# Four plain products ahead of the state products in the last batch's first attention chunk

## The chip, the cores and the metric

The kernel runs on one core of a Trainium2 chip. The metric is the device time of one execution in microseconds; "before" and "after" are two versions of the same kernel. The engines are called as in the profile: PE (TensorE, matrix products, with PEld for its weight loads), DVE (VectorE), ACT (ScalarE), POOL (GpSimd) and SP (SyncE, which here only issues DMAs). DMAs are issued from SP, ACT and POOL.

## The reference

Two blocks follow each other. First a causal linear attention with decay over 4 batches, 8 heads, 768 positions and head size 64, in which a state is carried from block to block:

```python
intra = einsum('bhic,bhjc->bhij', qb, kb) * Dmask        # scores, masked by lam ** (i - j)
intra = einsum('bhij,bhjd->bhid', intra, vb)
inter = einsum('bhid,bhde->bhie', qb * lam_pow, kv_state)
out[:, :, sl] = intra + inter
kv_state = lam_block * kv_state + einsum('bhsd,bhse->bhde', kb * rev_pow, vb)
```

The heads are joined to rows of 512. Then comes a Fourier mixing layer on these x (4 x 768 x 512), all in float32:

```python
mixed = real(fft(fft(x, axis=1), axis=2))
u = x + mixed
un = (u - mean(u)) / sqrt(var(u) + 1e-06)
return u + maximum(un @ w_ch1, 0) @ w_ch2                # 512 -> 2048 -> 512
```

## The kernel before

**Stages.** Each batch passes through a front: attention in six chunks of 128 rows (`attn`, with `attn_in` for loads and transposes and `attn_out` for the rest of a chunk), then `fft_ln`: folds of the rows with their mirrored rows on DVE, the transform along the sequence as products with a table (L516), the transform along the width (L529 to L534), the sum u (L599 to L603) and the normalization (`norm`, L546 to L577). The mirrored rows come back from DRAM by indirect DMAs: each chunk's rows x are stored from ACT (L365 to xa, L367 to xb), `mirror_a` and `mirror_b` gather them on POOL (L439, L445, L452).

**The plain feed-forward.** The normalized rows are handled in twelve pairs of 128-row tiles. The first four pairs (`PLAIN`) pass through `mlp`, the plain products: L636 is the first layer (eight or sixteen groups of four products into a PSUM bank), L644 on ACT or L642 on DVE the relu that empties the bank, L650 the second layer (for each of two tiles, eight or sixteen products accumulated in one bank), L661 and L662 on DVE add u and make y, and y goes to the output from SP (L623) or, for the mirrored tile, as a scatter from POOL (L625). PSUM has three banks for these (`pm`) and five for everything else (`pa`).

**The late pairs.** The other eight pairs are written to DRAM and handled at the end by `late`, with combined weights: `combine_weights` (L700, on DVE) forms sums of weight blocks, L713 to L716 those of the rows (us), L723 and L770 are the products and L750 to L762 and L736 to L743 the copies, sums and relus between them.

**The order of the work.** A part of the kernel is a Python generator that issues some instructions and then yields a number, its planned duration. `weave` runs a lead generator and, each time it yields d, issues work of the other generator until that one's planned time has caught up with a ratio of the lead's. So the number yielded decides how much plain work is issued at that place. In the last woven stretch the lead is the fronts of batches 1 to 3 (`fr`), and the other is the plain products left (`back`). A scheduler then sets the final order on each engine by readiness and issue order; `tc.keep_in_program_order(i)` holds an instruction at its place in the order of issue.

**The place of the change.** In `attn_out` the scores are L298 (k and q transposed, sixteen instructions), masked on DVE at L302 to sc, then comes `yield 1.5`. The state products are L315 (kd, made on POOL at L270, times v, into pu), copied or added to the state on DVE (L317, L320), then `yield 0.9`. Then po takes the state part (L328, not in chunk 0) and the scores part (L332, which reads sc). ACT copies po (L335), PE turns it (L348) and ACT copies it to x (L352, L353). In batch 3 (the last, B - 1) the plain products that lie beside chunks 0 and 1 are the L650 of the second pair's second half (`half[1][1]`, two tiles); beside chunks 2 to 5 lies the third pair's second half, and from there on the fourth pair.

Of the kernel before, what the change touches and what calls it, by code (L numbers as in the profile page):

```python
# [76 lines left out]
def kernel(  # L77
# [11 lines left out]
    B, H, S, D = q.shape  # L89
# [16 lines left out]
    HD = [slice(0, 64), slice(64, 128)]  # L106
# [36 lines left out]
    def psum_a(shape):  # L143
        return new(pa, shape, "pa")
# [101 lines left out]
    def attn(b):  # L246

        head = () if b - 1 in LEADS else attn_in(b, 0)
        for c in range(NC):
            yield from head  # L250
            head = attn_in(b, c + 1) if c < NC - 1 else attn_in(b + 1, 0) if b in LEADS else ()
            yield from attn_out(b, c, head)
# [36 lines left out]
    def attn_out(b, c, head):  # L289
        kT, qT, qs, kd, vt = ins.pop((b, c))  # L290
# [3 lines left out]
        mm = nc.tensor.matmul  # L294
# [8 lines left out]
            sc.append(t)  # L303
        if last and b - 1 in LEADS:
            mirror_a(b, pin=True)
        yield 1.5


        s_old, s_new = st[(c + 1) % 2], st[c % 2]
        if not last:  # L310
            pu = psum_a([128, HP, D])
            for hp in range(HP):
                for hi in range(2):
                    h = 2 * hp + hi
                    mm(pu[HD[hi], hp, :], lhsT=kd[:, h, :], rhs=vt[:, h, :], start=True, stop=True)  # L315
            if c == 0:
                nc.vector.tensor_copy(s_new, pu)  # L317
            else:
                nc.gpsimd.tensor_tensor(s_new, s_old, spow.broadcast_to([128, HP, D]), op=ALU.mult)
                nc.vector.tensor_tensor(s_new, s_new, pu, op=ALU.add)  # L320
            yield 0.9
# [3 lines left out]
        if c > 0:  # L325
            for hp in range(HP):
                for hi in range(2):
                    mm(po[HD[hi], hp, :], lhsT=s_old[HD[hi], hp, :], rhs=qs[HD[hi], hp, :],  # L328
                       start=(hp == 0), stop=False, skip_group_check=True)
        for hp in range(HP):  # L330
            for hi in range(2):
                mm(po[HD[hi], hp, :], lhsT=vt[:, 2 * hp + hi, :], rhs=sc[hi][:, hp, :],  # L332
                   start=(c == 0 and hp == 0), stop=(hp == HP - 1), skip_group_check=True)
# [99 lines left out]
    def mirror_a(b, pin=False):  # L433

        xa = xd[b][0]

        eo[b] = new_eo()
        for a, n in enumerate(BLK):
            i = gather(out=eo[b][a][1][0:n, 1, 0:DM], out_offset=None, in_=xa[:, :], in_offset=row_of(a, n))  # L439
            if pin:  # L440

                tc.keep_in_program_order(i)
        for t in range(2, HC):
            u = xs[b, HC + t] = new(xp, [128, DM], "x")
            i = gather(out=u[:, :], out_offset=None, in_=xa[:, :], in_offset=row_of(2 + t))  # L445
            if pin:
                tc.keep_in_program_order(i)
# [458 lines left out]
```

## Time and profile before

| | us |
|---|---|
| median of five runs | 822.7 (820.37 to 824.76) |
| profiled execution | 820.77 |
| its span, first to last instruction | 819.0 |
| PE busy in the span | 794.2 |
| DVE busy | 438.3 |
| ACT busy | 185.7 |
| POOL busy | 84.8 |

The granted TensorE clock was 0.999 of full speed over the span, so no part of the time is due to a slower clock. In the profile a line is that of the kernel before. The last batch's attention lies between about 286 and 357 us, its folds between 355 and 374, its transform and normalization up to about 420, and the late pairs from 428 to the end at 819. PE's float32 products are issued as two instructions each, with a weight load each; the counts in the profile are those of instructions. A row of a timeline gives its start, its length, engine, line, operation, output <- inputs, shape and count, and in brackets how long the engine stood idle before it and what ended that.

### The profile page before, as it was taken

The page shows a single profiled execution, that of the slowest core. Times are in us where ns is not written, and L with a number is a line of the kernel's source. Part 1 is how long each engine was busy: PE and PEld are TensorE (multiplying, and loading weights), DVE is VectorE, ACT ScalarE, POOL GpSimd, SP SyncE. Part 2 cuts the span into 40 slices and gives each one's busy share as a digit, 9 for nine tenths or more (in the row PEclk, how much of TensorE's full clock was granted, in tenths as well). Part 3 has the DMA queues.
Part 4 walks back from the last instruction along what each step waited for, and adds up shares of the span by engine and source line. Part 5 has one row for each costly group of instructions (what it writes and reads, how often), then busy time and mean ns, then how long its engine had stood idle before and what let it go on. Part 6 is the DMA issues. An engine that isn't in the chain of part 4 may idle for free.

```text
span 819.0 us, 11694 instructions
## 1 busy us (share of the span) xinstructions
PE 794.2 (97%) x4608; PEld 634.3 (77%) x4608; DVE 438.3 (54%) x1018; ACT 185.7 (23%) x448; POOL 84.8 (10%) x102
## 2 busy tenths in 40 slices
PE   6989899999999999999999999999999999999998
PEld 5767767767585857768648888888888888888886
DVE  6899798766743761364995541255313661146311
ACT  3755344225420211312002200022001210022100
POOL 3223340011011010220000000000000000000000
PEclk9999999999999999999999999999999999999999
DMA  9969524248741136530350011100111001110010
GB/s 253 258 126 274 171 90 129 65 117 200 198 125 51 53 63 130 130 122 26 94 165 38 1 53 51 52 1 1 64 40 52 0 1 39 33 33 0 1 39 26
DMA packets 126684, 68.88 MB, mean 84 GB/s; under 512 B 111150, under 2 KB 112174, under 8 KB 126630
## 3 DMA queue, kind: packets, MB, share of 16 engines
q1 hardware_dynamic: 121488, 55.67, 26.5%
q0 software_dynamic: 2112, 6.69, 2.4%
q10 hardware_dynamic: 3030, 5.78, 1.9%
q8 instruction: 36, 0.59, 0.3%
q14 instruction: 18, 0.15, 0.1%
HBM read 48.72 MB, written 19.40 MB: 83 GB/s over the span
## 4 chain that ended last, share of the span: by engine, by line
PE 80%; DVE 10%; issue 4%; DMA 3%; ACT 2%; POOL 1%; POOLq 0%; ACTq 0%; DVEq 0%
PE p L770 24%; PE p L723 24%; PE pm L650 10%; PE pm L636 8%; PE pa L332 3%; PE pa L516 3%; PE pa L298 2%; DMA x<-xb,ix 2%; PE pa L328 2%; PE pa L274 1%; PE pa L315 1%; DVE sc L302 1%; PE pa L348 1%; PE pa L279 1%; DVE stt L546 1%
## 5 line engine op out<-in xcount | busy, mean ns | idle before, releaser
L636 PE MATMUL pm<-ut,w 128*128 128x256 f32 x512 | 119.2, 382 | 0.0
L650 PE MATMUL pm<-w,hr 128*128 128x512 f32 x256 | 115.8, 597 | 0.1
L636 PEld LDWEIGHTS pm<-ut,w 128*128 128x128 f32 x512 | 94.4, 190 | 15.4 <-issue 3.6
L723 PE MATMUL p<-ur,w 128*128 128x256 f32 x384 | 93.8, 379 | 0.0
L650 PEld LDWEIGHTS pm<-w,hr 128*128 128x128 f32 x256 | 46.6, 190 | 49.5 <-issue 48.0
L723 PEld LDWEIGHTS p<-ur,w 128*128 128x128 f32 x384 | 73.0, 190 | 10.3 <-issue 0.5
L723 PE MATMUL p<-us,w1s 128*128 128x256 f32 x256 | 65.7, 379 | 0.0
L770 PE MATMUL p<-w,hs 128*128 128x256 f32 x256 | 58.0, 379 | 0.5 <-DVE y L791 0.5
L770 PE MATMUL p<-w2s,hs 128*128 128x256 f32 x256 | 57.9, 379 | 0.0
L770 PE MATMUL p<-w,ha 128*128 128x256 f32 x256 | 57.9, 379 | 0.0
L770 PEld LDWEIGHTS p<-w,hs 128*128 128x128 f32 x256 | 48.5, 190 | 7.5 <-DVE y L791 0.9
L770 PEld LDWEIGHTS p<-w2s,hs 128*128 128x128 f32 x256 | 48.6, 190 | 6.6
L723 PEld LDWEIGHTS p<-us,w1s 128*128 128x128 f32 x256 | 48.6, 190 | 6.6
L770 PEld LDWEIGHTS p<-w,ha 128*128 128x128 f32 x256 | 48.6, 190 | 6.6
L625 POOL DMA_INDIRECT out_dram<-y,ix x12 | 11.8, 987 | 402.0 <-DVE y L796 342.6
L750 ACT COPY ha<-p 128x256 f32<-128x256 f32 x32 | 11.9, 372 | 169.1 <-PE p L723 139.4
L761 DVE TENSOR_TENSOR ha<-p,ha 128x256 f32<-128x256 f32 x32 | 13.6, 424 | 45.2 <-ACT ha L760 45.2
L298 PEld LDWEIGHTS pa<-qT,kT 64*128 64x128 f32 x384 | 26.0, 193 | 13.2 <-ACT qT L281 7.2
L302 DVE TENSOR_TENSOR sc<-pa,decay 128x512 f32<-128x512 f32 x48 | 31.4, 682 | 8.9 <-PE pa L298 8.9
L332 PE MATMUL pa<-sc,v 128*64 128x128 f32 x384 | 31.5, 281 | 3.4 <-DVE sc L302 3.4
L298 PE MATMUL pa<-qT,kT 64*128 64x128 f32 x384 | 30.7, 292 | 3.2 <-ACT qT L281 2.9
L723 PE MATMUL p<-ur,w1s 128*128 128x256 f32 x128 | 32.8, 379 | 0.0
(144 smaller groups left out, 1123.4 us busy)
## 6 DMA issues: line engine op xcount, KB each, us to landing
raw<-in_moe_w_ch_dram SPq DMA_DIRECT2D x32, 512.0 KB, 4.3
k<-in_k_dram SPq DMA_DIRECT2D x24, 256.0 KB, 5.1
q<-in_q_dram SPq DMA_DIRECT2D x24, 256.0 KB, 5.8
v<-in_v_dram SPq DMA_DIRECT2D x24, 256.0 KB, 4.7
ud<-x SPq DMA_DIRECT2D x16, 256.0 KB, 2.3
utd<-e SPq DMA_DIRECT2D x64, 64.0 KB, 2.2
u<-ud SPq DMA_DIRECT2D x16, 256.0 KB, 2.5
ur<-utd SPq DMA_DIRECT2D x6, 512.0 KB, 3.7
```

The source lines that it names most:

```text
L298: mm(pss[hi][:, hp, :], lhsT=kT[HD[hi], hp, :], rhs=qT[HD[hi], hp, :], start=True, stop=True)
L302: nc.vector.tensor_tensor(t, pss[hi], decay[:, hi::2, :], op=ALU.mult)
L328: mm(po[HD[hi], hp, :], lhsT=s_old[HD[hi], hp, :], rhs=qs[HD[hi], hp, :], start=(hp == 0), stop=False, skip_group_check=True)
L332: mm(po[HD[hi], hp, :], lhsT=vt[:, 2 * hp + hi, :], rhs=sc[hi][:, hp, :], start=(c == 0 and hp == 0), stop=(hp == HP - 1), skip_group_chec ...
L516: mm = nc.tensor.matmul(ps[0:m, n, :], lhsT=piece(a, i, n), rhs=cs[0:rows, a, i in (2, 3), n, :], start=(a == 0), stop=(a == 1))
L625: nc.gpsimd.indirect_dma_start(out=out.rearrange("b s d -> (b s) d"), out_offset=row_of(2 + HC * (b + 1) + T - HC), in_=y[:, :], in_offset ...
L636: nc.tensor.matmul(ps, lhsT=w1[:, c, 128 * fc:128 * fc + 128], rhs=ut[:, c, :], start=(c == 0), stop=(c == KO - 1))
L650: nc.tensor.matmul(ps, lhsT=hr[(fc - f0) // 4][:, fc % 4, 128 * i:128 * i + 128], rhs=w2[:, fc, :], start=(fc == f0), stop=(fc == f1 - 1))
L723: nc.tensor.matmul(ps, lhsT=s2.A[a][:, kt, 128 * i:128 * i + 128], rhs=U[b][:, kt, :], start=(first and kt == 0), stop=(kt == 1), skip_gro ...
L750: nc.scalar.copy(a11, two(X))
L761: V.tensor_tensor(a22, two(Z), a22, op=ADD)
L770: nc.tensor.matmul(ps, lhsT=h[a][:, s, i, :], rhs=s2.B[b][:, i, :], start=(first and i == 0), stop=(i == HF - 1), skip_group_check=True)
```

## The change

The number yielded between scores and state products becomes 5.0 instead of 1.5 in chunk 0 of batch 3, and the first state product of that chunk is held at its place in the order of issue.

```diff
-        yield 1.5
+
+        yield 5.0 if (b, c) == (B - 1, 0) else 1.5
...
-                    mm(pu[HD[hi], hp, :], lhsT=kd[:, h, :], rhs=vt[:, h, :], start=True, stop=True)
+                    i = mm(pu[HD[hi], hp, :], lhsT=kd[:, h, :], rhs=vt[:, h, :], start=True, stop=True)
+                    if (b, c, h) == (B - 1, 0, 0):
+                        tc.keep_in_program_order(i)
```

In the built programs every engine issues the same instructions as before, and the order is the same up to this chunk. From here on it differs as follows (lines of the kernel before).

- PE: between L298 and L315 of chunk 0 stand seven products of L650 instead of three. In chunk 1, L315 comes ahead of four products of L650 instead of behind them, and none stand behind its L332. From there to the last L348 of the attention there are fourteen products of L650 instead of twelve, behind it two instead of four, then L636. Before the transform's products on the second block of rows stand 28 products of L636 instead of 23, and between the first of the three parts of the transform along the width and L723 there are 27 instead of 32.
- DVE: L661 and L662 of the second pair's first tile stand ahead of L317 of chunk 0, those of the third pair's first tile ahead of L285 of chunk 5, and those of its second tile ahead of the first eight folds (L426 to L430, on the rows that `mirror_a` gathers), each instead of behind.
- POOL: the scatter L625 of that last tile (the third pair's second) stands ahead of the two gathers L452 of batch 3 instead of behind them.
- ACT: one relu (L644) stands ahead of the copy L466 of the folds instead of behind it. SP: no difference.

## The prediction

> **What bounds the kernel now.** I read the page first: TensorE (PE) is busy nearly all the time and carries most of the chain that ended last, so a microsecond counts only if PE stands still in it, or if another engine holds up its last stage.
>
> ```profile
> PE 794.2 (97%) x4608; PEld 634.3 (77%) x4608; DVE 438.3 (54%) x1018; ACT 185.7 (23%) x448; POOL 84.8 (10%) x102
> PE 80%; DVE 10%; issue 4%; DMA 3%; ACT 2%; POOL 1%; POOLq 0%; ACTq 0%; DVEq 0%
> ```
>
> Next the PE timeline where batch 3's first chunk runs (start, length, instructions; a product counts as two):
>
> ```profile
> 288.98 2.84 PE L650 MATMUL pm<-w,hr 128*128 128x512 f32 x6
> 291.75 0.69 PE L315 MATMUL pa<-v,kd 128*64 128x64 f32 x16
> 294.01 0.43 PE L332 MATMUL pa<-sc,v 128*64 128x128 f32 x2 [1.58 <-DVE sc L302]
> ...
> 296.48 3.60 PE L650 MATMUL pm<-w,hr 128*128 128x512 f32 x8
> ```
>
> PE waits 1.58 us for the masked scores, which VectorE (DVE) finishes late. This is the largest such wait. The next PE wait is at 371.97, for the folds of batch 3 (0.96 us); behind it come the timelines of POOL, DVE and ACT:
>
> ```profile
> 114.47 6.21 POOL L452 DMA_INDIRECT x<-xb,ix  x1 [0.30 <-issue]
> ...
> 360.46 0.94 POOL L452 DMA_INDIRECT x<-xb,ix  x1 [4.83 <-DMA xb<-xn]
> 361.71 0.95 POOL L452 DMA_INDIRECT x<-xb,ix  x1 [0.30 <-issue]
> 362.96 0.99 POOL L625 DMA_INDIRECT out_dram<-y,ix  x1 [0.30 <-issue]
> ```
> ```profile
> 355.44 0.69 DVE L426 TENSOR_TENSOR fe<-fo,xn 128x512 f32<-128x512 f32 x1 [3.86 <-DMA fo<-xa,ix]
> 356.17 0.69 DVE L427 TENSOR_TENSOR fo<-fo,xn 128x512 f32<-128x512 f32 x1
> ...
> 363.70 0.69 DVE L426 TENSOR_TENSOR fe<-x,x 128x512 f32<-128x512 f32 x1 [2.54 <-DMA x<-xb,ix]
> ...
> 428.43 0.41 DVE L662 TENSOR_TENSOR y<-pm,x 128x256 f32<-128x256 f32 x1
> ```
> ```profile
> 428.85 0.37 ACT L750 COPY ha<-p 128x256 f32<-128x256 f32 x1 [29.72 <-DVE y L662]
> 429.72 0.42 DVE L752 TENSOR_TENSOR ha<-p,ha 128x256 f32<-128x256 f32 x1 [0.89 <-ACT ha L750]
> ```
>
> The last rows matter most. The first copy of the last stage (L750) starts when DVE has ended L662 (428.84), not when its PE bank is full; it ends at 429.22, and PE's first products with us, which write that bank again, start at 429.46. PE has 0.24 us to spare. DVE has no pause to give: from 403.65 to 428.84 it is busy 25.15 of 25.19 us. So two chains of equal length meet here: PE's products, and gather, folds, transform, normalization and weight combinations, mostly on DVE. A stall filled on PE helps only if the second chain comes earlier too.
>
> **Step 1, the stall.** Four more products (eight instructions of 0.43 us) stand before L315. From the rows: 288.98 + 2.77 (six instructions) + 3.44 (eight more) puts L315 at 295.19, + 0.61 (its length at 305.17) L332 at 295.80. The masked scores end at 294.56, so the wait is gone; the last of the four needs the relu that DVE ends at 293.36 and would start at 294.14, so it does not wait either. Then 1.03 for L332 and 0.49 + 0.44 for the transposes, now uninterrupted: the next L650 at 297.76. Before, PE had done the same work at 296.48 + 3.44 = 299.92: 2.16 ahead, 1.58 of the wait and 0.58 of the split runs. With the same rows for chunk 1, whose state products L315 now stand ahead of its plain ones, L636 comes at 309.00 instead of 311.36: 2.36 ahead. POOL's kd for chunk 1 follows L315 and would be ready at about 297, needed at 302.8; the L317 copy moves behind y (about 297.6, needed at 307): both are covered by products.
>
> **Step 2, more products before the last chunk's store.** The weave hands out plain work earlier from here on. As built, 14 and not 12 L650 products lie between chunk 1 and the last L348: + 1.72. The last L348 comes at 356.32 - 2.36 + 1.72 = 355.68, 0.64 earlier.
>
> **Step 3, queues.** SP's order does not change. On POOL the scatter L625 now stands before both L452 gathers, and on DVE L661/L662 (the y it waits for) before the first folds instead of after them. L661 waits for the last L650: 355.68 + 0.44 + 1.72 = 357.84; + 0.20, + 0.75: y ends at 358.79. The eight folds queued behind it start at about 358.71 (their gather, landed at 355.44 before, is long there), and take 4.08, as before: to 362.79. POOL starts L625 0.28 after y (326.46 to 326.75 before): 359.07. The gathers wait behind it, and DVE's second folds, and then PE, for them.
>
> Here is the cost that no row shows directly. Both POOL issues fall beside folds that read two SBUF tiles back to back. The nearest row is the 6.21 us at 114.47: DVE ran such instructions without a pause until L470 waited for ACT (119.77), and POOL ended 0.94 later, just one undisturbed issue. So POOL got in at DVE's first pause. The folds have one: L426 to L427 takes 0.73 (355.44 to 356.17), against 0.61 at 363.70. I take entry there, the row nearest in kind: L625 at 359.32, + 0.99 + 0.30 the gather asks at 360.61, inside the folds again, and enters at the second such pause, 361.33. Lower bound: no hold, 359.07 + 1.29 = 360.36; a row speaks for it too, since at 354.64 a POOL issue took 0.99 while L426 ran beside it, but POOL had begun first. Upper bound: held until the folds end, 362.79 + 1.29 = 364.08. The scatter's own transfer (3.2 from issue to landing) ahead of the gather's could add up to 0.3; I take none. Against 360.46 the gather is 0.87 later (-0.10 to +3.62).
>
> [...]
>
> **Step 4, folds to transform.** DVE's second folds start 3.24 after the gather, at 364.57. PE's L636 groups run dry of banks: the sixth waits for the L642 that DVE runs inside the folds, 4.33 after their start (368.90), while PE is there at 366.5: a new PE wait of about 2.4 us. It costs nothing by itself, as the folds would stop PE a group later anyway: L516 on the second block at 364.57 + 8.27 = 372.84 instead of 371.97. On ACT one more relu (L644) stands before the fold's small copy L466; PE has filled its bank by 363.1 and the copy is due at 366: covered. One more product of L516 stands behind the block (0.33): the transform hands over to DVE 1.2 later than at 384.01.
>
> **Step 5, the junction.** PE now has five L636 products (2.16) fewer between the transform and L723, so it is there 2.16 - 1.20 = 0.96 early and waits. DVE's chain has the same instructions in it and ends 1.2 later; less the 0.24 to spare, PE's first products with us start 0.96 later. Behind this nothing changes.
>
> Sum: 1.20 - 0.24 = +0.96, about +1.0 us. The profiled execution took 820.77 (span 819.0 and 1.8 around it), so 821.7 for its like; the median of the five runs is 1.9 higher, 822.7, which gives 823.7. About 0.3%, 2.5 us, can be told from no change, so this is "same".
>
> **Rivals.**
> - The folds do not hold POOL (chance 0.27): -0.10 + 0.01 + 0.33 - 0.24 = 0.0, 822.7. For it: the issue at 354.64. Against it: 114.47.
> - Slower, one mechanism (0.17): POOL gets no pause until the folds end. The gather is 3.62 late, + 0.33 - 0.24 = +3.7, 826.4. It exceeds 2.5 us once the gather starts later than 362.8. For it: 5.3 us without entry at 114.47. Against it: the 0.12 pause in the folds.
> - The stall does not go (0.05): the added products wait for their relu on DVE, busy with normalization just then. Without the 2.36 gained, everything is later: +3.3, 826.0.
> - Faster (0.06): PE's own chain decides, with L750 free of DVE. Both PE waits gone is 2.36 + 0.96 = 3.3, 819.4. Against it: if only the earlier store counted, the second chain would be 0.64 - 0.33 earlier, + 0.24: a gain of 0.55 at most while L750 waits for L662.
>
> **How the numbers follow.** The forecast has 0.45 and its own range 823.1 to 824.5 (entry one pause earlier or later, the scatter's 0.3). The medians themselves scatter by about 1 us (820.37 to 824.76 over five runs). The faster case and the tail below no change are left out, the held POOL is kept: 821.2 to 826.4. Held POOL, a stall that stays, less what of them stays under 2.5 us: slower 0.19; faster 0.06; the rest, 0.75, same.
>
> **What would show it.** Step 1: no wait for sc at L332, its start near 295.8, L636 near 309.0. Step 2: last L348 near 355.7. Step 3: L625 longer than 1.1 or late against y, the first L452 starting or ending after 361.5. Step 4: a PE wait before an L636 group near 366.5, L516 near 372.8. Step 5: PE idle before its third pair of L723, with L750 still released by L662. I am wrong if POOL's issues are 0.95 long and on time (then no change), if L625 or L452 lasts 4 us (then slower), or if L750 starts while DVE is still at L700.

## The result, and the profile after

The changed kernel takes 824.07 us (median of 33 runs, 821.49 to 827.59), the kernel before 821.97 (58 runs): ratio 1.0027, 95% interval 1.0018 to 1.0035. That is slower by some 2.2 us (2.1 between the medians), "same" by the 0.3% of the prediction, and within its range. The number was right to 0.4 us, but the loss is twice the +1.0 of the sum, and its place was not the one forecast.

In the new profile a line of `late` stands 3 higher than before: L723 is L726, L750 is L753, L662 is L665; L302 stays. The profiled execution took 824.51 us (span 822.7). Executions reach the last batch's first chunk at different times, so from here I count from the transposes of q ahead of it (L279), which stand at 286.49 before and 287.22 after, and call this t. The span ends at t = 532.51 before and 535.48 after: +2.97. Spans are given to 0.1 us, so differences between such ends hold to about 0.1.

Two rows of PE before the change, the point from which t counts and the beginning of the last stage, whose first two products (called X and Y below) stand in one row of eight instructions:

```profile
286.49 0.60 PE L279 MATMUL pa<-ident,q 128*128 128x128 f32 x4
...
427.74 1.89 PE L723 MATMUL p<-ur,w 128*128 128x256 f32 x8
```

The timeline of PE in the changed kernel (start, length, line, instructions, and in brackets the idle time ahead and what ended it):

```profile
287.22 0.60 PE L279 MATMUL pa<-ident,q 128*128 128x128 f32 x4
...
296.43 1.04 PE L335 MATMUL pa<-sc,v 128*64 128x128 f32 x16
...
369.15 1.99 PE L639 MATMUL pm<-ut,w 128*128 128x256 f32 x8 [1.65 <-DVE hr L645]
...
426.98 1.03 PE L726 MATMUL p<-ur,w 128*128 128x256 f32 x4
430.57 1.71 PE L726 MATMUL p<-ur,w 128*128 128x256 f32 x4 [2.56 <-DVE y L665]
432.07 1.91 PE L726 MATMUL p<-us,w1s 128*128 128x256 f32 x4
433.78 1.30 PE L726 MATMUL p<-ur,w 128*128 128x256 f32 x4
434.92 1.03 PE L726 MATMUL p<-us,w1s 128*128 128x256 f32 x4
```

Two things are to be seen. The wait for the scores is gone, and PE reaches the last stage (its first product, X) at t = 139.76 instead of 141.25, 1.49 earlier. But there its second product (Y, a12 times b21) stands still for 2.56 us, until DVE has ended the last plain y (L665). Then twelve instructions, which before took 0.86 us per four, take 4.35 instead of 2.59. The windows view of the same kernel tells why (window, its length, busy time of PE, PEld, DVE, ACT and POOL, then the granted clock):

```profile
430.60:430.80 0.20, 0.20 (x1) 0.20 (x2) 0.00 (x0) 0.00 (x0) 0.09 (x1) 1.00 0.78 287
430.80:431.00 0.20, 0.20 (x2) 0.17 (x2) 0.00 (x0) 0.00 (x0) 0.20 (x1) 0.80 1.07 420
431.00:434.20 3.20, 3.20 (x9) 2.46 (x8) 0.72 (x2) 0.18 (x1) 0.79 (x1) 0.50 0.75 291
434.20:434.40 0.20, 0.20 (x2) 0.19 (x1) 0.00 (x0) 0.20 (x1) 0.00 (x0) 0.67 0.00 0
```

The granted clock is 0.50 for 3.4 us, from about 430.9 to 434.3, right after the idle time. So +2.97 is 1.24 of wait (Y starts at t = 143.35; before it was 142.11, worked out as the start of the row of eight at 427.74 plus 0.86) and some 1.7 of half clock.

The timelines of POOL, DVE and ACT of the changed kernel, for steps 3 and 5:

```profile
359.94 1.19 POOL L628 DMA_INDIRECT out_dram<-y,ix  x1 [4.96 <-DMA xb<-xn]
361.43 1.08 POOL L455 DMA_INDIRECT x<-xb,ix  x1 [0.30 <-issue]
362.81 0.99 POOL L455 DMA_INDIRECT x<-xb,ix  x1 [0.30 <-issue]
```
```profile
364.77 0.69 DVE L429 TENSOR_TENSOR fe<-x,x 128x512 f32<-128x512 f32 x1 [1.13 <-DMA x<-xb,ix]
...
427.87 0.69 DVE L717 TENSOR_TENSOR us<-ur,us 128x512 f32<-128x512 f32 x1
...
430.01 0.41 DVE L665 TENSOR_TENSOR y<-pm,x 128x256 f32<-128x256 f32 x1
```
```profile
428.09 0.37 ACT L753 COPY ha<-p 128x256 f32<-128x256 f32 x1 [29.72 <-DMA out_dram<-y]
```

The scatter L628 is 1.19 long, not 0.99; the gather behind it starts at t = 74.21 instead of 73.97, the second folds at 77.55 instead of 77.21, and the last y ends at 143.20 instead of 142.35, 0.85 later. The copy L753 does not wait for y: it starts 1.11 after PE's first product, while DVE is still at L717.

### The profile page after: what moved, and what is told of

Its sections match the earlier page's. It is cut to its first block, busy times and chain, and to the rows that moved or that the text cites. A ratio compares the mean times of both kernels' runs of the same rounds, so it can differ in the third digit from the quotient of the medians.

```text
span 822.7 us, 11692 instructions
## 1 busy us (share of the span) xinstructions
PE 795.3 (97%) x4608; PEld 635.2 (77%) x4608; DVE 438.0 (53%) x1018; ACT 186.6 (23%) x448; POOL 85.2 (10%) x102
## 5 line engine op out<-in xcount | busy, mean ns | idle before, releaser
L639 PE MATMUL pm<-ut,w 128*128 128x256 f32 x512 | 119.2, 383 | 1.7 <-DVE hr L645 1.7
L639 PEld LDWEIGHTS pm<-ut,w 128*128 128x128 f32 x512 | 94.3, 190 | 16.8 <-issue 2.9
L726 PE MATMUL p<-ur,w 128*128 128x256 f32 x384 | 94.9, 382 | 2.6 <-DVE y L665 2.6
L726 PEld LDWEIGHTS p<-ur,w 128*128 128x128 f32 x384 | 73.5, 191 | 13.5 <-issue 3.4
L726 PE MATMUL p<-us,w1s 128*128 128x256 f32 x256 | 66.6, 383 | 0.0
L726 PEld LDWEIGHTS p<-us,w1s 128*128 128x128 f32 x256 | 49.2, 192 | 6.9
L628 POOL DMA_INDIRECT out_dram<-y,ix x12 | 12.1, 1007 | 406.1 <-DVE y L799 343.6
L753 ACT COPY ha<-p 128x256 f32<-128x256 f32 x32 | 11.9, 372 | 169.1 <-PE p L726 139.4
L302 DVE TENSOR_TENSOR sc<-pa,decay 128x512 f32<-128x512 f32 x48 | 31.4, 682 | 13.6 <-PE pa L298 13.6
L298 PEld LDWEIGHTS pa<-qT,kT 64*128 64x128 f32 x384 | 26.0, 193 | 13.2 <-ACT qT L281 7.2
L298 PE MATMUL pa<-qT,kT 64*128 64x128 f32 x384 | 30.7, 292 | 3.2 <-ACT qT L281 2.9
L270 POOL TENSOR_TENSOR kd<-k,decay 128x512 f32<-128x512 f32 x20 | 23.1, 1155 | 99.1 <-PE pa L316 59.8
L335 PE MATMUL pa<-sc,v 128*64 128x128 f32 x384 | 31.1, 280 | 1.8 <-DVE sc L302 1.8
```

Source lines behind the costliest of these rows:

```text
L270: nc.gpsimd.tensor_tensor(kd, kt, kpow, op=ALU.mult)
L298: mm(pss[hi][:, hp, :], lhsT=kT[HD[hi], hp, :], rhs=qT[HD[hi], hp, :], start=True, stop=True)
L302: nc.vector.tensor_tensor(t, pss[hi], decay[:, hi::2, :], op=ALU.mult)
L628: nc.gpsimd.indirect_dma_start(out=out.rearrange("b s d -> (b s) d"), out_offset=row_of(2 + HC * (b + 1) + T - HC), in_=y[:, :], in_offset ...
L639: nc.tensor.matmul(ps, lhsT=w1[:, c, 128 * fc:128 * fc + 128], rhs=ut[:, c, :], start=(c == 0), stop=(c == KO - 1))
L726: nc.tensor.matmul(ps, lhsT=s2.A[a][:, kt, 128 * i:128 * i + 128], rhs=U[b][:, kt, :], start=(first and kt == 0), stop=(kt == 1), skip_gro ...
```

## The experiments

My theory was now: (A) the changed order turns the three `pm` banks so that Y gets the bank which the last y is read from, PE waits there, and the clock falls behind the wait. In the built kernels, before: the last plain product stands in bank 6, Y takes bank 7 and Z, later, bank 6; after: the last plain product and Y both have bank 7. The last stage takes banks 0, 7 and 6 in both; it is the last plain tile that has moved. Rivals: (B) DVE's lateness, from the scatter ahead of the gathers, sets the end whatever the bank; (C) the half clock has nothing to do with the wait.

**The bank alone.** A tile that takes bank 7 for itself, ahead of Y:

```diff
+            if (i, j) == (0, 0):
+                V.memset(bank()[0:1, 0:1], 0.0)
             prod(Y, "a12", "b21", i, True)
```

> The changed kernel with one thing more: a one-element memset takes the PSUM bank that the last plain tile's y is read from, so that the second product of the last stage (Y, L726) gets another bank. Theory A (that bank and the fall of the clock behind the wait for it make the loss): no idle time of TensorE at its second pair of L726 (2.56 us in the changed kernel), granted clock 1.00 between 426 and 440 (0.50 for 3.4 us there), TensorE ahead of the kernel before by some 0.8 us, median 819.5 to 821.5 us. Theory B (VectorE's chain up to the last y, late by 0.8 us from the scatter ahead of the gathers, sets the end by itself): the wait moves to a later product, 823 to 824 us. Theory C (the half clock comes whatever TensorE does there): the wait goes, the clock still falls, about 821.5 to 822 us.

Measured: 820.68 us against 822.13, ratio 0.9978 (0.9963 to 0.9992). The timelines of PE and DVE with the free bank:

```profile
426.39 1.89 PE L726 MATMUL p<-ur,w 128*128 128x256 f32 x8
428.13 1.10 PE L726 MATMUL p<-us,w1s 128*128 128x256 f32 x4
```
```profile
427.29 0.69 DVE L717 TENSOR_TENSOR us<-ur,us 128x512 f32<-128x512 f32 x1
...
429.44 0.41 DVE L665 TENSOR_TENSOR y<-pm,x 128x256 f32<-128x256 f32 x1
```

X and Y are one row of eight now, and the products with us run at 428.13, 1.7 us before y ends (429.85). Nothing in PE's path needs y but the bank. The span ends at t = 531.16, 1.35 ahead of the kernel before, and one run of twelve has a mean clock of 0.998 or less. B falls at this place: y ends 0.96 later than before (t = 143.31), and once the bank is free that costs nothing. What PE needs of DVE here is us: L717 ends at 427.98, and the products with us start 0.15 behind it, just as PE gets there (426.39 plus twice 0.86). So DVE's lateness is covered, but only just.

**The other way round.** The same two lines in the kernel before push Y onto its busy bank.

> The kernel before, with the same one-element memset: here it pushes Y off the free bank and onto the one that the last plain tile's y is read from. Theory A (bank): TensorE, that is done with X at 428.60, waits at Y for VectorE, that is done at 428.84: a new wait of 0.4 to 0.7 us, and the end 0.4 to 0.7 us later, 822.5 to 822.8 us against 822.1; if waits of half a microsecond can start a half clock as well, half of the runs a further 1.7 us later. Rival (the memset itself and the new turn of the banks help or harm in some other way): equal to the kernel before, or a change of more than 1 us without a wait at Y.

Measured: 823.38 us against 822.49, ratio 1.0011 (0.9993 to 1.0029): the medians do not tell it from no change. The profile does. PE with the busy bank in the kernel before:

```profile
429.51 1.03 PE L723 MATMUL p<-ur,w 128*128 128x256 f32 x4
430.75 1.10 PE L723 MATMUL p<-ur,w 128*128 128x256 f32 x4 [0.21 <-DVE p L752]
```
```profile
430.19 0.41 DVE L662 TENSOR_TENSOR y<-pm,x 128x256 f32<-128x256 f32 x1
430.59 0.06 DVE L752 MEMSET p<- 1x1 f32 x1
```

Y starts 1.24 after X instead of 0.86, 0.38 late, and the span ends at t = 532.99, 0.48 late. PE's row names the memset (L752), the last DVE event ahead of the start, but in the built program Y waits for y (L662), which ended at 430.60. Y starts 0.15 behind that, as it does in the changed kernel (430.42 to 430.57). The wait comes with the bank, and goes with it.

**Work in place of the wait.** Needless products ahead of X, on its bank, whose result X overwrites, three of them in one kernel and one in another:

```diff
+            if (i, j) == (0, 0):
+                for _ in range(3):
+                    prod(X, "a11", "b11", 0, True)
             prod(X, "a11", "b11", i, True)
```

> The changed kernel with three needless products (12 instructions, 2.59 us at full clock, their result overwritten by the next) on the bank of X ahead of X, so that TensorE works where it waited 2.56 us for the bank of Y. Y can start no earlier than before this edit. Theory A: Y's pair starts at the same time within 0.2 us, no half clock behind it, 12 instructions of L726 behind Y take 2.6 us, not 4.35, and the end is 1.7 us earlier: 822.2 to 822.6 us median, and no run with a mean clock under 0.999. Theory C: the clock falls as before and the time stays at 824.0, or rises by up to 2.6 us.

Measured: 822.91 us, ratio 1.0004 (0.9988 to 1.0021), two runs of twelve with a mean clock of 0.998 or less (expected were 822.2 to 822.6 and no such run). PE's row, X and Y in it, has no gap:

```profile
426.30 4.70 PE L726 MATMUL p<-ur,w 128*128 128x256 f32 x20
430.84 1.03 PE L726 MATMUL p<-us,w1s 128*128 128x256 f32 x4
```

The span ends at t = 533.84, +1.33, with the clock at 1.00: doing 2.6 us of useless work instead of waiting makes the execution 1.6 us shorter than the profiled one of the changed kernel, and the median 1.2 us lower. What is left, 1.3 us, is the late start of Y.

**The dose.** One needless product leaves 1.7 us of idle time; a y done five times over makes it longer:

```diff
-                tt(y[:, 0:HM], ps[:, 0:HM], u[:, 0:HM], op=ALU.add)
+                for _ in range(5 if (b, g, i) == (*PLAIN[3], 1) else 1):
+                    tt(y[:, 0:HM], ps[:, 0:HM], u[:, 0:HM], op=ALU.add)
```

> The changed kernel with one needless product (4 instructions, 0.86 us) ahead of X, its result overwritten: TensorE's idle time at Y shrinks from 2.56 to 1.7 us, and Y still can't start earlier. At full clock the time is that of the changed kernel at full clock (822.6 us). What is asked is how often the clock falls: with 2.56 us of idle, 44 of 71 runs had a mean clock of 0.998 or less; in four kernels without this wait 12 of 48. [...]

> The changed kernel with the add of the last plain tile's first half (L664) done five times over instead of once, with the same result: VectorE's y ends 4 x 0.335 = 1.34 us later and TensorE idles 3.9 us at Y. At full clock 1.34 us more than the changed kernel, 823.9 us. If idle time makes the clock fall, it falls in nearly every run (10 of 12 or more at 0.998 or less) and the median is 825.3 to 826.5 us. If the falls have nothing to do with this wait, 7 of 12 at most and 824.5 to 825.3 us.

Measured: 822.92 us (1.0002, 0.9988 to 1.0017) with one product, 826.88 (1.0047, 1.0032 to 1.0063) with the long wait. The five adds lie 0.46 apart, not 0.335, so the wait became 4.39 us and the time passed the 826.5 expected. PE with the one product, then PE with the long wait:

```profile
430.54 1.10 PE L726 MATMUL p<-ur,w 128*128 128x256 f32 x4 [1.70 <-DVE y L665]
```
```profile
426.91 1.03 PE L727 MATMUL p<-ur,w 128*128 128x256 f32 x4
432.33 2.05 PE L727 MATMUL p<-ur,w 128*128 128x256 f32 x4 [4.39 <-DVE y L666]
434.17 1.91 PE L727 MATMUL p<-us,w1s 128*128 128x256 f32 x4
435.88 1.91 PE L727 MATMUL p<-ur,w 128*128 128x256 f32 x4
437.58 1.35 PE L727 MATMUL p<-us,w1s 128*128 128x256 f32 x4
```

How many runs had a mean clock of 0.998 or less, by the idle time at Y:

| idle at Y | kernels | runs at 0.998 or less |
|---|---|---|
| none | free bank, three products, and two below (both, catching up) | 12 of 48 |
| 1.70 us | one product | 2 of 12 |
| 2.56 us | the change, without its pin, and two with the scatter moved | 44 of 71 |
| 4.39 us | long wait | 11 of 11 |

With 2.56 us the share is well above that without a wait, with 4.39 us every run has a fall, and in the profiles of the change and of the long wait the half clock comes with it: C falls. With 1.70 us the share is no higher than with none (2 of 12 against 12 of 48), so of the idle times tried 2.56 us is the shortest with a larger share; no run lies between. A mean clock counts falls anywhere in the execution, and Y is not the only place: the kernel before, which has no wait at Y, has 39 of 92, and with the busy bank 8 of 12.

**The pin.** The changed kernel with the yield alone:

```diff
-                    i = mm(pu[HD[hi], hp, :], lhsT=kd[:, h, :], rhs=vt[:, h, :], start=True, stop=True)
-                    if (b, c, h) == (B - 1, 0, 0):
-                        tc.keep_in_program_order(i)
+                    mm(pu[HD[hi], hp, :], lhsT=kd[:, h, :], rhs=vt[:, h, :], start=True, stop=True)
```

> The changed kernel without its pin: the yield alone stays. Every engine's order of instructions is the same with and without the pin. So: 824.0 us, within 1 us of the changed kernel's median; the same wait of 2.5 to 2.6 us at the second pair of L723 (here the lines stand 3 lower or fewer), and like the changed kernel more than half of its runs with a mean clock under 0.999. If the pin acts in a way that the order doesn't show: up to 2 us less.

Measured: 824.63 us, ratio 1.0029 (1.0012 to 1.0047), nine of twelve runs at 0.998 or less. The pin does nothing: the order is the same on every engine, and the time too. The profiled execution without it is worth more: the same order and the same wait, with the clock at 1.00.

```profile
425.43 1.03 PE L724 MATMUL p<-ur,w 128*128 128x256 f32 x4
429.01 1.10 PE L724 MATMUL p<-ur,w 128*128 128x256 f32 x4 [2.56 <-DVE y L663]
429.95 1.03 PE L724 MATMUL p<-us,w1s 128*128 128x256 f32 x4
```

It ends at t = 533.79: the changed order costs +1.28 us without a fall of the clock, and +2.97 with one.

**The scatter on POOL.** Two kernels. In the first I held the store back in a list and emptied the list where `mirror_b` is called for the last batch:

```diff
+                if b == B - 1:
+                    while held:
+                        store(*held.pop())
...
+                if (b, g, i) == (*PLAIN[2], 1):
+                    held.append((b, T, y))
+                else:
+                    store(b, T, y)
```

> The changed kernel with the scatter of the plain tile (POOL, L628) put behind the gathers that stand ahead of the second folds, as it stands in the kernel before. Theory A: gathers 0.4 to 1.4 us earlier, second folds and the last y of VectorE 0.3 to 0.9 us earlier, the wait at Y shorter by that much and the half clock perhaps still there: 822.5 to 823.8 us. Theory B (this place is the whole loss): 821.7 to 822.0 us. If POOL's order costs nothing: 824.0 us.

As built, the list is filled only after that point, so this kernel leaves the scatter out altogether (128 rows of the output are never written). Measured: 824.31 us, above the 822.5 to 823.8 expected, ratio 1.0026 (1.0005 to 1.0048), nine of twelve runs at 0.998 or less; the profiled execution, at full clock, ends at t = 533.04, 0.75 before the one without the pin.

In the second the list is emptied at the start of the folds (`fold_b`), and the scatter and the two gathers are pinned in this order:

```diff
+            while b == B - 1 and held:
+                tc.keep_in_program_order(store(*held.pop()))
...
-            gather(out=u[:, :], out_offset=None, in_=xd[b][1][:, :], in_offset=row_of(2 + t))
+            i = gather(out=u[:, :], out_offset=None, in_=xd[b][1][:, :], in_offset=row_of(2 + t))
+            if b == B - 1:
+                tc.keep_in_program_order(i)
```

> The changed kernel with that one scatter on POOL put behind the two gathers by pins, all other engines' orders unchanged. Leaving the scatter out moved VectorE's last y 0.75 us forward. Theory: the gathers are issued 0.9 to 1.3 us earlier, VectorE's second folds and last y 0.3 to 0.75 us earlier, the wait at Y stays 2.0 to 2.6 us (TensorE, too, comes earlier), with it the half clock in about half of the runs: 823.0 to 823.8 us. Rival (the place of the scatter costs nothing, its transfer does): 824.0 us.

Measured: 823.68 us, ratio 1.0012 (0.9998 to 1.0026). POOL, DVE and PE:

```profile
364.32 1.11 POOL L455 DMA_INDIRECT x<-xb,ix  x1 [5.67 <-DMA xb<-xn]
365.73 0.96 POOL L455 DMA_INDIRECT x<-xb,ix  x1 [0.30 <-issue]
367.00 1.13 POOL L634 DMA_INDIRECT out_dram<-y,ix  x1 [0.30 <-DVE fe L432]
```
```profile
367.81 0.69 DVE L429 TENSOR_TENSOR fe<-x,x 128x512 f32<-128x512 f32 x1 [0.55 <-DMA x<-xb,ix]
```
```profile
372.19 1.99 PE L645 MATMUL pm<-ut,w 128*128 128x256 f32 x8 [1.07 <-DVE hr L651]
...
433.60 1.10 PE L735 MATMUL p<-ur,w 128*128 128x256 f32 x4 [2.56 <-DVE y L671]
```

L279 is at 290.88 here. The second folds start at t = 76.93 instead of 77.55, the wait at L639 shrinks from 1.65 to 1.07, and the last stage, wait and all, comes 0.6 earlier (X at 139.13, Y at 142.72). The first gather starts 0.77 earlier (t = 73.44 instead of 74.21), which is enough for all of it. So the place of the scatter costs some 0.6 us at the end (533.22 against 533.79); the rival, that only its transfer costs, falls. The half clock of this execution is elsewhere: 0.50 for 3.4 us from about 29.1, behind two waits for the scores in the first batches (2.06 and 1.22 us with 0.43 of work between them). L279 stands 3.7 us later than in the changed kernel's execution, which is why no spans are compared here without t.

**Both.** The scatter behind the gathers and the free bank.

> Both edits: the scatter behind the gathers, and the bank of Y freed by the memset. Theory A (TensorE sets the last stage once the bank is free, and VectorE's lateness is then covered): the same as with the free bank alone within 0.5 us, 820.2 to 821.0 us. Rival (VectorE's chain still shows through): 0.4 to 0.8 us earlier than with the free bank alone, 819.8 to 820.2 us.

Measured: 820.08 us, ratio 0.9975 (0.9957 to 0.9993). The end is at t = 530.37, 0.79 before the free bank alone. The rival had the size; the place is the folds, as above (X at 139.00 instead of 139.85, the wait at L639 0.93 instead of 1.78), not the junction.

**The added products without the rest.** The four products stay in chunk 0, and the two yields of chunk 1 go to 0, so that the weave has caught up by chunk 2:

```diff
-        yield 5.0 if (b, c) == (B - 1, 0) else 1.5
+        yield 5.0 if (b, c) == (B - 1, 0) else 0.0 if (b, c) == (B - 1, 1) else 1.5
...
-        yield 2.0
+        yield 0.0 if (b, c) == (B - 1, 1) else 2.0
```

> The four products are still moved into the first chunk of the last batch, but the second chunk's two yields are set to 0, so that the plain work handed out catches up there and all engines' orders from that chunk on are those of the kernel before; banks too. Theory A: the wait for the scores stays away, everything behind is 2.36 us earlier, no wait for a bank at the last stage: 819.4 to 820.2 us. Rival (something else than TensorE sets the beginning of the folds and the last stage, so that an earlier TensorE only waits there): 821.5 to 822.2 us, with a new wait of up to 2.4 us between chunk 1 and the last stage.

Measured: 820.55 us, ratio 0.9979 (0.9961 to 0.9997). PE and DVE, with L279 at 287.66:

```profile
426.42 1.89 PE L726 MATMUL p<-ur,w 128*128 128x256 f32 x8
428.15 1.03 PE L726 MATMUL p<-us,w1s 128*128 128x256 f32 x4
```
```profile
427.11 0.41 DVE L665 TENSOR_TENSOR y<-pm,x 128x256 f32<-128x256 f32 x1
```

Everything comes earlier together: the last y ends at t = 139.86 instead of 142.35, X starts at 138.76 instead of 141.25, the span ends at 530.04, 2.47 earlier. This is the gain that step 1 had worked out as 2.36. The median lies 0.35 above theory A's range: five of the twelve runs have a mean clock of 0.998 or less, and the seven at 1.000 have a median of 819.70.

All of it in one table, from the profiled executions (t from L279) and the runs:

| kernel | X at t | Y at t | end at t | against before | median of runs |
|---|---|---|---|---|---|
| before | 141.25 | 142.11 | 532.51 | | 821.97 |
| the change, half clock | 139.76 | 143.35 | 535.48 | +2.97 | 824.07 |
| without the pin | 139.72 | 143.30 | 533.79 | +1.28 | 824.63 |
| scatter behind | 139.13 | 142.72 | 533.22 | +0.71 | 823.68 |
| bank free | 139.85 | 140.71 | 531.16 | -1.35 | 820.68 |
| both | 139.00 | 139.86 | 530.37 | -2.14 | 820.08 |
| catching up in chunk 1 | 138.76 | 139.62 | 530.04 | -2.47 | 820.55 |

Where X and Y are one row of eight, Y is X plus 0.86. The medians come from three sets of runs, in which the kernel before had 821.97, 822.13 and 822.49. The last three kernels are faster than the kernel before (their intervals lie below 1), and their medians are at least 3.4 us below that of the change. Which of them is the fastest is not settled: the intervals of their ratios overlap.

## Why the prediction was right or wrong

**Step 1, right.** No wait for sc at L335, which starts at t = 9.21 (predicted 295.80, 9.31); the gain carries through, as the kernel that catches up shows.

**Step 2, right.** The last L351 starts at 356.51, t = 69.29, predicted 69.19.

**Step 3, mechanism right, term too big.** The scatter now stands ahead of the gathers and is 1.19 long, 0.20 more than before; if the folds held it, then by no more than that. It starts 0.28 behind y, without the 0.25 that I had added there, and the first gather takes 1.08 and starts 0.24 later than before, not 0.87. The second hold that I had added from the pause at 356.17 (0.72) is hardly there. With the scatter moved back the folds come 0.62 earlier, the end some 0.6. The truth lies between my forecast and the rival "no hold"; "held until the folds end" is far off.

**Step 4, right, with step 3's smaller size.** The new wait ahead of an L639 group is there, 1.65 long (predicted 2.4). As forecast it costs nothing by itself: the second block starts at 373.05, t = 85.83 (predicted 86.35), 0.05 behind the end of the fold that it reads (L478, 373.00). What costs is that the folds are late: with the scatter moved the wait shrinks by 0.6, and PE reaches the last stage 0.6 earlier. DVE's first sum behind the transform (L602) starts 0.67 later than before, t = 98.19 instead of 97.52 (predicted 1.2): 0.34 from the folds and 0.33 from the added product of the transform.

**Step 5, wrong.** The number was near: +0.96 predicted, +1.28 measured at full clock. The reason failed: "L750 waits for L662". I read that from 428.85 standing 0.01 behind the end of L662. In every kernel here without needless products the copy starts 1.10 to 1.11 after PE's first product (427.74 to 428.85 before, 426.98 to 428.09 after, 426.42 to 427.53 with chunk 1 catching up): X's product released it, and the profile's releaser was the last event by coincidence. The built program agrees: this copy waits for X's product, for some DMAs, and on DVE for nothing later than a transpose of the normalization (L577). The 0.24 between its end and the products with us is no slack against y either: both count from X, and with chunk 1 catching up it is 0.25. My own test, "wrong if L750 starts while DVE is still at L700", came out against me in kind: L753 starts beside L717. PE's products with us were free of y all along, so the rival "PE's own chain decides" had the right mechanism, and with the bank free the kernel is faster (-1.35; -3.3 was too much, since PE reaches the last stage only 1.4 earlier). What stood in its place was not in my list: a PSUM bank handed from the last plain tile to Y, which no row of the trace before shows, since there Y got a free one. The built programs show it without a run: before, Y waits for the y of the last plain tile but one; after, for that of the last.

That the number came near is luck in part, as two errors offset each other. y ends 0.85 later, not 1.20. But nothing is to be taken off: 0.39 comes on top, because before Y did not wait for y at all (it started at t = 142.11, y ended at 142.35, and 0.15 pass between the end of y and a Y that waits for it). 0.85 and 0.39 are the 1.24 by which Y is late.

**The sum.** To +1.28 comes the clock. It was 0.998 or less in 20 of 35 executions of the changed kernel, and in 39 of 92 of the kernel before. Runs with a mean clock of 1.000 have a median of 822.59 after (15 runs) and 821.70 before (34): +0.9. The rest of the +2.2 goes with the larger share of runs with a fall; 20 of 35 against 39 of 92 is a difference that chance alone would bring about in one case of six, so these counts do not settle that part. I had no term for it, and the near hit of 823.7 is in part luck here too: it was the median of five runs, 822.7, plus 1.0, while 58 runs gave 821.97.

**Open.** Why the clock falls in so many runs of the kernel before. Its wait of 1.58 us for the scores is a candidate, but 1.70 us of idle time at Y gave 2 of 12 only, and the kernel that catches up, without either wait, has 5 of 12. The early waits seen with the scatter moved are another. It wasn't tried. Nor does any run show what held POOL for 6.21 us at 114.47.

## What to carry to other kernels

When a change moves the order of products, look at which PSUM banks the next stage takes first, and who reads them last: here two stages follow each other on the same banks, the second product of the next one stood still for 2.56 us until the last reader of its bank had ended, and one unused tile took that wait away. The built program names bank and wait before any run. A releaser 0.01 us ahead of a start is no proof: compare the delay from the other producer in several places first. And give back at once, beside the place, the work that a yield pulls forward, or every queue behind it changes its order.

## What the runs showed of the hardware

In the changed kernel's profiled execution PE stood idle for 2.56 us at Y, and behind that the granted clock was 0.50 for 3.4 us (430.9 to 434.3). That cost about 1.7 us: 4.35 instead of 2.59 for twelve instructions. It happened at Y in one of the four profiled executions that had this wait; in 44 of 71 runs of these four kernels the mean clock was 0.998 or less, against 12 of 48 of the kernels without it. After 1.70 us it was 2 of 12, no more than without. After 4.39 us it was 11 of 11, and in the profiled one the clock was 0.50 for 6.8 us, from 431.4 to 438.2, beginning while PE still waited (Y started at 432.33). Why the clock falls behind the same wait in one execution and not in another is not shown by any run here.

POOL's issues of the scatter and the gathers at the last folds took 0.94 to 0.99 us before, when DVE's first folds were over (359.52), and 0.99 to 1.19 after, beside these folds: a hold of some 0.2 at most, far from the 6.21 us at 114.47 on which I had built step 3.
